# A decode step fed by one load queue: first load cut by partitions, x turned by TensorE, wo in five pieces

## The chip, the cores and the metric

The kernel runs on one core of a Trainium2 chip. The metric is device time in microseconds (us), the median of several executions. A core has five engines that run side by side: TensorE (PE in the profile; its weight loads are PEld), VectorE (DVE), ScalarE (ACT), GpSimd (POOL) and SyncE (SP), which here only issues loads. Loads are carried out by 16 DMA engines.

## The reference, cut to what matters

One token (x has 576 numbers) goes through two mixers whose outputs are added to x. All tensors are bfloat16.

```
xn = layernorm(x)
# A: attention over the last W = 4096 of 65536 cached positions, 32 query heads, 16 KV heads of 128
q  = xn @ wq                              # [576] x [576, 4096]
p  = softmax(q . k_cache[last W] / sqrt(128));  o = p . v_cache[last W]
A  = o @ wo                               # [4096] x [4096, 576]
# B: gated MLP
z  = gelu(xn @ w_in)                      # [576] x [576, 4608];  z1, z2 = halves
B  = (z1 * (w_sp * layernorm(z2) + b_sp)) @ w_out
out = x + A + B
```

What is read: 33.6 MB of K and V, 4.7 MB wq, 5.3 MB w_in, 2.7 MB w_out and 4.7 MB wo. Each byte is used once.

## The kernel before, in words

**The loads.** Every large load is issued by SP in the order of the program (lines 99 to 111): wq in two tiles of 5 and 4 half rows per partition; K0 and K1; w_in in three tiles; then K2 to K7 alternating with V0 to V5; V6, V7; w_out; wo in pieces of 10, 8, 6, 4, 2 and 2 rows per partition. A K or V tile (`load_kv`) is two heads, 128 partitions of 16 KB each. All tiles come from one ring of seven buffers (`ring`), so a load waits until the reader of an earlier tile in its buffer is done. Besides, transfers report their landing on eight counters that are used in turn, and a load waits until the transfer before it on its counter has landed. SP issues in order: a load that waits holds all behind it.

**x.** ScalarE's queue issues four small loads (lines 114 to 120): x as 64 partitions of 9 numbers (`x64`), x as one row (`xrow`, used at the end to add x to the output), and two scalars (`spb`). PE spreads x64 over 128 partitions by a matmul with a 0/1 matrix `rmat` that POOL copies from the identity (lines 137 and 194), so that partition p holds the nine numbers of p // 2. Lines 197 to 219 compute the layernorm and write `XT`.

**The work.** With XT, 36 matmuls give q (`qps`, L227); copies, matmuls and scalings lay it out as `Qb` (L236 to L255). Then a loop goes over sixteen half tiles of K, four per group: VectorE transposes half a K tile (`t_half`, L268), PE computes scores (`s_half`, L277); after each group VectorE takes the maximum (L298), ScalarE the exponentials (L305), VectorE and ScalarE transpose them (L315, L321), and PE multiplies with V (`pv`, L344). The MLP's input matmuls (L380) run after the first group. At the end the last group's output is normalised and laid out as `Y` (L354 to L372), and matmuls add w_out's and wo's products to two accumulators (L467), wo's pieces in the order in which they land. Two casts and one store end the program (L492 to L494). The order on each engine is that of the program text.

Of the kernel before, what the change touches and what calls it, by code (L numbers as in the profile page):

```python
# [9 lines left out]
BF16 = mybir.dt.bfloat16  # L10
# [4 lines left out]
D = 576  # L15
# [3 lines left out]
SK = 65536  # L19
W = 4096  # L20
# [6 lines left out]
TP = 2 * NT  # L27
# [7 lines left out]
NS = 9  # L35
# [4 lines left out]
def kernel(  # L40
# [14 lines left out]
    nc = tc.nc  # L55
    P = nc.NUM_PARTITIONS
# [4 lines left out]
    const = ctx.enter_context(tc.tile_pool(name="const", bufs=1))  # L61
# [10 lines left out]
    x_flat = A_x.flatten_outer_dims()  # L72


    def ring_tile(name, rows, width):
        t = ring.tile([P, SLOT], BF16, name=name, tag="ring")
        return t[:, 0:rows * width].rearrange("p (s c) -> p s c", c=width)

    def load_halves(src, lo, n, name):

        v = ring_tile(f"{name}{lo}", n, src.shape[1] // 2)
        rows = src.rearrange("r (e c) -> (r e) c", e=2).rearrange("(p s) c -> p s c", s=NS)
        nc.sync.dma_start(v, rows[:, lo:lo + n, :])
        return [(lo + s, v[:, s, :]) for s in range(n)]

    def load_kv(src, m, name):

        t = ring.tile([P, SLOT], BF16, name=f"{name}{m}", tag="ring")
        v = t[:, 0:TP * DH]
        nc.sync.dma_start(v, src[0, 2 * m:2 * m + 2, SK - W:SK, :].rearrange("h (r t) d -> r h (t d)", t=TP))  # L90
        return v.rearrange("p (t d) -> p t d", d=DH)

    def load_n(src, per, lo, n, name):
        v = ring_tile(f"{name}{lo}", n, D)
        nc.sync.dma_start(v, src.rearrange("(p t) n -> p t n", t=per)[:, lo:lo + n, :])
        return [(lo + t, v[:, t, :]) for t in range(n)]

    K, V = {}, {}
    wq_sb = load_halves(A_wq, 0, 5, "wq") + load_halves(A_wq, 5, 4, "wq")
    for m in range(2):  # L100
        K[m] = load_kv(A_k_cache, m, "k")
    win_sb = sum((load_halves(B_w_in, lo, 3, "win") for lo in (0, 3, 6)), [])
    for m in range(2, NP):
        K[m] = load_kv(A_k_cache, m, "k")
        V[m - 2] = load_kv(A_v_cache, m - 2, "v")
# [1 line left out]
        V[m] = load_kv(A_v_cache, m, "v")  # L107
    wout_sb = load_n(B_w_out, NF, 0, NF, "wout")
    wo_sb = []
    for n in (10, 8, 6, 4, 2, 2):  # L110
        wo_sb += load_n(A_wo, 32, len(wo_sb), n, "wo")


    x64 = const.tile([64, NS], BF16, name="x64")
    nc.scalar.dma_start(x64[:], x_flat.rearrange("o (m j) -> (o m) j", j=NS))
    xrow = const.tile([1, D], BF16, name="xrow")
    nc.scalar.dma_start(xrow[:], x_flat)
    spb = const.tile([1, 2], BF16, name="spb")
    nc.scalar.dma_start(spb[:, 0:1], B_w_sp.flatten_outer_dims()[0:1, 0:1])
    nc.scalar.dma_start(spb[:, 1:2], B_b_sp.flatten_outer_dims()[0:1, 0:1])  # L120


    ident = const.tile([P, P], BF16, name="ident")
# [7 lines left out]
    ones_b = const.tile([1, P], BF16, name="ones_b")  # L131
    nc.vector.memset(ones_b[:], 1.0)
    ps_x = ps_m.tile([P, 512], FP32, name="ps_x", tag="m")
    nc.vector.memset(ps_x[:], 0.0)
    qps = ps_a.tile([P, 512], FP32, name="qps", tag="a")
    nc.vector.memset(qps[:], 0.0)
    rmat = const.tile([64, P], BF16, name="rmat")
    nc.gpsimd.tensor_copy(rmat[:].rearrange("p (r h) -> p r h", h=2),
                          ident[0:64, 0:64].unsqueeze(2).to_broadcast([64, 64, 2]))
    mask = const.tile([P, 2], FP32, name="mask")  # L140
    nc.vector.reduce_sum(mask[:], ident[:].rearrange("p (r h) -> p h r", h=2), axis=AXX)
    mask4 = const.tile([P, 4], FP32, name="mask4")
# [32 lines left out]
    for n in range(2):  # L175
        t = const.tile([P, TP, 16, 2], BF16, name=f"pz{n}")
# [3 lines left out]
    for n in range(2):  # L180
        t = ps_s.tile([P, 2, 512], FP32, name=f"S{n}")
# [9 lines left out]
    nc.gpsimd.memset(mb[:], 0.0)  # L191


    nc.tensor.matmul(ps_x[:, 0:NS], lhsT=rmat[:], rhs=x64[:], start=True, stop=True)  # L194
    x_col = const.tile([P, NS], FP32, name="x_col")
    stat = const.tile([P, 2], FP32, name="stat")
    nc.vector.tensor_copy(x_col[:], ps_x[:, 0:NS])
# [27 lines left out]
    for s, wv in wq_sb:  # L225
        for g in range(4):
            nc.tensor.matmul(  # L227
                qps[32 * g:32 * g + 2, :], lhsT=XT[:, s, :], rhs=wv[:, 512 * g:512 * (g + 1)],
                start=(s == 0), stop=(s == NS - 1), tile_position=(0, 32 * g),
# [12 lines left out]
    for k in range(4):  # L242
        for be in range(4):
            nc.tensor.matmul(
                qps2[:, k, be, :].rearrange("p (r g) -> p r g", r=2),
                lhsT=q_rep[0:NR, 2 * k + be // 2, be % 2].rearrange("p a d -> p (a d)"),
                rhs=idq, start=True, stop=True)
# [181 lines left out]
    for j in range(2 * NP):  # L429
        g, o = divmod(j, GK)  # L430
# [7 lines left out]
        if g > 0 and o == 1:  # L438
            if g > 1:
                sm_b(g - 1)  # L440
            else:
# [3 lines left out]
                for n, pool in enumerate((ps_a, ps_b)):  # L445
                    t = pool.tile([P, 512], FP32, name=f"acc{n}", tag="ab"[n])
                    acc.append(t[32 * n:32 * n + 1, 0:CW])
                    nc.tensor.matmul(acc[n], lhsT=ones_b[:, 0:1], rhs=xrow[:, CW * n:CW * (n + 1)],
                                     start=True, stop=False, tile_position=(0, 32 * n))
# [75 lines left out]
```

## Time and profile before

| | |
|---|---|
| median of 3 runs | 127.74 us (127.64 to 127.87) |
| profiled execution | 127.7 us, span 125.9 us |
| busy in the span | PE 67.8 us, DVE 77.3, ACT 33.6, POOL 8.2 |
| read from memory | 50.96 MB, 405 GB/s over the span |
| DMA packets | 4127, 534 of them under 512 B |
| x64: issued, landed, first use | 0.74, 9.27, 9.40 us |
| XT ready, first qps matmul | 13.03 us |
| last K tile landed | 90.96 us |
| Y written | 116.67 us |
| last wo piece landed | 122.83 us |

The span runs from the first to the last recorded instruction; the run's time has 1.8 us more around it. The page has strips of 40 equal slices of 3.15 us: a digit is the busy share of a slice in tenths, and below the DMA line stands what was moved in GB/s. The chain of waits is read from the last instruction backwards, each step to what released it. "SPq" is SP's queue: the time in which it issues a load. A row of the waits gives who waited for whom, the total in us, how many times, and the longest.

### The profile page before, as it was taken

How to read it: one execution, taken by the hardware profiler on the slowest of the kernel's cores; microseconds unless marked ns; L12 is line 12 of the kernel's file. 1: busy time of each engine (PE TensorE's matmuls, PEld its weight loads, DVE VectorE, ACT ScalarE, POOL GpSimd, SP SyncE). 2: the span in 40 equal slices, each digit the busy share in tenths (PEclk: the TensorE clock that was granted, in tenths of full speed). 3: DMA queues.
4: the chain of work that ended last, by engine and by line, in shares of the span. 5: the costliest groups of instructions: out<-in, count | busy, mean ns of one | idle time of the engine just before them, and what ended most of it. 6: DMA issues, size and time to landing. Idle time of an engine off the chain costs nothing.

```text
span 125.9 us, 1614 instructions
## 1 busy us (share of the span) xinstructions
PE 67.8 (54%) x618; PEld 30.9 (25%) x618; DVE 77.3 (61%) x149; ACT 33.6 (27%) x85; POOL 8.2 (7%) x28
## 2 busy tenths in 40 slices
PE   0002841089999977069356049648039711187861
PEld 0001301021299922014111012411012511024530
DVE  6704135999353896793898298899098967005001
ACT  1200011000036590000441930260950183910001
POOL 3991000000000000100000000000000000000000
PEclk9999999999996557856999959967756995559999
DMA  4999999999999999999999999999999999999950
GB/s 130 417 427 437 432 422 442 419 426 433 435 429 427 442 416 416 437 437 432 437 422 432 437 427 432 432 416 437 437 424 437 427 426 453 409 416 415 419 226 0
DMA packets 4127, 51.06 MB, mean 406 GB/s; under 512 B 534, under 2 KB 536, under 8 KB 1048
## 3 DMA queue, kind: packets, MB, share of 16 engines
q1 hardware_dynamic: 4034, 50.96, 95.3%
q8 instruction: 5, 0.08, 0.2%
q10 hardware_dynamic: 86, 0.00, 0.0%
q14 instruction: 2, 0.02, 0.0%
HBM read 50.96 MB, written 0.00 MB: 405 GB/s over the span
## 4 chain that ended last, share of the span: by engine, by line
DMA 56%; PE 16%; DVE 14%; ACT 7%; issue 3%; SPq 1%; POOL 0%; ACTq 0%
DMA k<-in_A_k_cache_dram 43%; DMA x<-in_A_x_dram 7%; DMA wo<-in_A_wo_dram 7%; DVE kT L268 6%; PE ops L344 6%; PE S L277 5%; ACT PT L321 4%; PE qps L227 3%; ACT pz L305 2%; DVE Qb L255 2%; DVE pt L315 2%; DVE q_rep L238 1%; ACT q_rep L236 1%; DVE on L358 1%; PE lps L327 1%
## 5 line engine op out<-in xcount | busy, mean ns | idle before, releaser
L277 PE MATMUL S<-kT,Qb 128*8 128x512 bf16 x128 | 32.5, 638 | 29.0 <-DVE kT L268 29.0
L268 DVE STREAM_TRANSPOSE kT<-k 128x1024 f32<-128x1024 f32 x32 | 36.9, 1212 | 6.9 <-DMA k<-in_A_k_cache_dram 6.8
L305 ACT ACTIVATE pz<-S,nm 64x1024 bf16<-64x1024 f32 x8 | 11.3, 1409 | 45.1 <-DVE nm L301 30.4
L321 ACT COPY PT<-pt 32x64 f32<-32x64 f32 x64 | 18.9, 296 | 14.3 <-DVE pt L315 13.6
L277 PEld LDWEIGHTS <-Qb 128*8 128x8 bf16 x128 | 6.4, 96 | 48.4 <-issue 45.4
L344 PE MATMUL ops<-v,PT 128*16 128x512 bf16 x128 | 11.7, 451 | 3.5 <-ACT PT L321 3.5
L315 DVE STREAM_TRANSPOSE pt<-pz 128x1024 bf16<-128x1024 bf16 x8 | 9.4, 1214 | 4.2 <-ACT pz L305 4.2
L380 PEld LDWEIGHTS <-win 128*128 128x128 bf16 x162 | 10.1, 169 | 0.9 <-issue 0.9
L380 PE MATMUL zps<-XT,win 128*128 128x2 bf16 x162 | 10.2, 202 | 0.0
L354 DVE SCALAR_TENSOR_TENSOR om<-ops,rs,dmask 128x512 f32<-128x512 f32 x4 | 3.0, 742 | 7.1 <-PE ops L344 7.1
L298 DVE TENSOR_REDUCE mx<-S 128x1 f32<-128x1024 f32 x4 | 4.9, 1222 | 3.8 <-PE S L277 3.8
L344 PEld LDWEIGHTS <-PT 128*16 128x16 bf16 x128 | 5.0, 98 | 7.4 <-ACT PT L321 4.1
L467 PE MATMUL acc<-wo,Y 128*1 128x288 bf16 x64 | 4.7, 285 | 1.7 <-DMA wo<-in_A_wo_dram 1.6
L194 PE MATMUL ps_x<-x,rmat 64*128 64x9 bf16 x1 | 0.2, 164 | 9.4 <-DMA x<-in_A_x_dram 9.4
L236 ACT CAST q_rep<-qps 128x512 bf16<-128x512 f32 x2 | 1.2, 585 | 14.7 <-DVE q_rep L238 14.7
L227 PE MATMUL qps<-wq,XT 128*2 128x512 bf16 x36 | 4.0, 626 | 1.0 <-DVE XT L218 1.0
L492 DVE CAST res<-acc 1x288 bf16<-1x288 f32 x1 | 0.4, 446 | 6.6 <-PE acc L467 6.6
L358 DVE TENSOR_REDUCE on<-om 128x128 f32<-128x512 f32 x4 | 4.1, 1036 | 0.1
L238 DVE CAST q_rep<-qps 128x512 bf16<-128x512 f32 x2 | 1.4, 692 | 4.6 <-PE qps L227 3.9
L327 PE MATMUL lps<-lx,lsum 128*128 128x1 f32 x8 | 2.2, 343 | 3.2 <-DVE Y L372 3.2
L493 ACT CAST res<-acc 1x288 bf16<-1x288 f32 x1 | 0.4, 389 | 12.7 <-PE acc L467 12.7
L467 PEld LDWEIGHTS <-Y 128*1 128x1 bf16 x64 | 2.8, 83 | 3.4 <-issue 2.5
(90 smaller groups left out, 44.6 us busy)
## 6 DMA issues: line engine op xcount, KB each, us to landing
k<-in_A_k_cache_dram SPq DMA_DIRECT2D x8, 2048.0 KB, 24.3
v<-in_A_v_cache_dram SPq DMA_DIRECT2D x8, 2048.0 KB, 24.8
win<-in_B_w_in_dram SPq DMA_DIRECT2D x3, 1728.0 KB, 23.3
wout<-in_B_w_out_dram SPq DMA_DIRECT2D x1, 2592.0 KB, 30.6
wq<-in_A_wq_dram SPq DMA_DIRECT2D x1, 2560.0 KB, 8.7
wq<-in_A_wq_dram SPq DMA_DIRECT2D x1, 2048.0 KB, 13.0
wo<-in_A_wo_dram SPq DMA_DIRECT2D x1, 1440.0 KB
wo<-in_A_wo_dram SPq DMA_DIRECT2D x1, 1152.0 KB
```

What stands on the lines that cost most here:

```text
L227: nc.tensor.matmul(qps[32 * g:32 * g + 2, :], lhsT=XT[:, s, :], rhs=wv[:, 512 * g:512 * (g + 1)], start=(s == 0), stop=(s == NS - 1), tile ...
L268: nc.vector.transpose(dst[:, 1024 * n:1024 * (n + 1)], src[:, 1024 * n:1024 * (n + 1)])
L277: nc.tensor.matmul(S[g % 2][32 * i:32 * i + 8, hf, :], lhsT=Qb[:, 2 * m + hd, be].rearrange("p a h -> p (a h)"), rhs=kv[:, be // 2, be % 2 ...
L298: nc.vector.tensor_reduce(out=mx[:, 0:1], in_=s[:], op=ALU.max, axis=mybir.AxisListType.XY)
L305: nc.scalar.activation(p[lo:hi, :, :, hd], s[lo:hi].rearrange("p a (t r) -> p (a t) r", r=16), ACT.Exp, bias=nm[lo:hi, 0:1], scale=SCALE, ...
L315: nc.vector.transpose(dst[:, 1024 * n:1024 * (n + 1)], src[:, 1024 * n:1024 * (n + 1)])
L321: nc.scalar.copy(PT4[32 * a:32 * a + 32, i % 2, i // 2, :], pt4[32 * i:32 * i + 32, :, a])
L327: nc.tensor.matmul(lps[:, 0:1], lhsT=lsum[:].rearrange("p q c x h -> p (q c x h)"), rhs=lx[:, g:g + 1], start=True, stop=True)
L344: nc.tensor.matmul(ops[32 * q:32 * q + 16, :], lhsT=d["PT"][:, pr, t0:t0 + 4].rearrange("p t x h -> p (t x h)"), rhs=V[2 * g + pr][:, t0:t ...
L358: nc.vector.reduce_sum(on[:], om[:].rearrange("p c d -> p d c"), axis=AXX)
L380: nc.tensor.matmul(zps[:, :, t], lhsT=wt[:, t, :], rhs=XT[:, s, :], start=(s == 0 and t == 0), stop=(s == NS - 1 and t == NF - 1), skip_gr ...
L467: nc.tensor.matmul(acc[n], lhsT=lhs[:, col:col + 1], rhs=wv[:, CW * n:CW * (n + 1)], start=False, stop=last, tile_position=(0, 32 * n))
```

## The change

- The first wq load has two half rows per partition, not five, and goes out in four transfers by partitions: every eighth from 0, every eighth from 4, every fourth from 2, every second from 1 (16, 16, 32, 64 partitions). The next wq loads have four and three half rows.
- `xrow` and the two scalars are issued by SP between the second and the third wq load. ScalarE's queue issues no load. `x64` and `rmat` are gone: VectorE copies xrow into `xtw`, one partition with 9 x 64 x 2 numbers, and nine matmuls with one column each spread it over the partitions.
- K0, K1 and the three w_in tiles go out in two transfers each, the even and the odd partitions.
- wo comes in pieces of 14, 9, 5, 3 and 1.
- The program has 40 transfers in place of 33. The loads' order of tiles, the ring and all later work stay; there are three wq tiles now, so the last w_in tile is the eighth in the ring.

```diff
-    def load_halves(src, lo, n, name):
+    def load_halves(src, lo, n, name, parts=((0, 1),)):
         v = ring_tile(f"{name}{lo}", n, src.shape[1] // 2)
         rows = src.rearrange("r (e c) -> (r e) c", e=2).rearrange("(p s) c -> p s c", s=NS)
-        nc.sync.dma_start(v, rows[:, lo:lo + n, :])
+        for p0, step in parts:
+            nc.sync.dma_start(v[p0:P:step], rows[p0:P:step, lo:lo + n, :])
...
-    def load_kv(src, m, name):
+    def load_kv(src, m, name, step=1):
...
-        nc.sync.dma_start(v, src[0, 2 * m:2 * m + 2, SK - W:SK, :].rearrange("h (r t) d -> r h (t d)", t=TP))
+        rows = src[0, 2 * m:2 * m + 2, SK - W:SK, :].rearrange("h (r t) d -> r h (t d)", t=TP)
+        for hd in range(step):
+            nc.sync.dma_start(v[hd:P:step], rows[:, hd:2:step, :])
...
-    wq_sb = load_halves(A_wq, 0, 5, "wq") + load_halves(A_wq, 5, 4, "wq")
+    wq_sb = load_halves(A_wq, 0, 2, "wq", ((0, 8), (4, 8), (2, 4), (1, 2)))
+    wq_sb += load_halves(A_wq, 2, 4, "wq")
+    xrow = const.tile([1, D], BF16, name="xrow")
+    nc.sync.dma_start(xrow[:], x_flat)
+    spb = const.tile([1, 2], BF16, name="spb")
+    nc.sync.dma_start(spb[:, 0:1], B_w_sp.flatten_outer_dims()[0:1, 0:1])
+    nc.sync.dma_start(spb[:, 1:2], B_b_sp.flatten_outer_dims()[0:1, 0:1])
+    wq_sb += load_halves(A_wq, 6, 3, "wq")
     for m in range(2):
-        K[m] = load_kv(A_k_cache, m, "k")
-    win_sb = sum((load_halves(B_w_in, lo, 3, "win") for lo in (0, 3, 6)), [])
+        K[m] = load_kv(A_k_cache, m, "k", 2)
+    win_sb = sum((load_halves(B_w_in, lo, 3, "win", ((0, 2), (1, 2))) for lo in (0, 3, 6)), [])
...
-    for n in (10, 8, 6, 4, 2, 2):
+    for n in (14, 9, 5, 3, 1):
         wo_sb += load_n(A_wo, 32, len(wo_sb), n, "wo")
-    x64 = const.tile([64, NS], BF16, name="x64")
-    nc.scalar.dma_start(x64[:], x_flat.rearrange("o (m j) -> (o m) j", j=NS))
...
-    rmat = const.tile([64, P], BF16, name="rmat")
-    nc.gpsimd.tensor_copy(rmat[:].rearrange("p (r h) -> p r h", h=2),
-                          ident[0:64, 0:64].unsqueeze(2).to_broadcast([64, 64, 2]))
...
-    nc.tensor.matmul(ps_x[:, 0:NS], lhsT=rmat[:], rhs=x64[:], start=True, stop=True)
+    xtw = const.tile([1, NS, D // NS, 2], BF16, name="xtw")
+    nc.vector.tensor_copy(xtw[:], xrow[:].rearrange("p (m j) -> p j m", j=NS).unsqueeze(3).to_broadcast([1, NS, D // NS, 2]))
+    for j in range(NS):
+        nc.tensor.matmul(ps_x[:, j:j + 1], lhsT=xtw[:, j].rearrange("p m h -> p (m h)"), rhs=ones_b[:, 0:1],
+                         start=True, stop=True)
```

More of the change, by code (lines that the diff above doesn't have):

```diff
@@ L109 @@
     wo_sb = []
-    for n in (10, 8, 6, 4, 2, 2):
+    for n in (14, 9, 5, 3, 1):
         wo_sb += load_n(A_wo, 32, len(wo_sb), n, "wo")
-    x64 = const.tile([64, NS], BF16, name="x64")
[L115 to L120, printed above, removed]
     ident = const.tile([P, P], BF16, name="ident")
```

## The prediction

> **What bounds the kernel now.** I read the strip of the page first, then the DMA rate by stage, then the chain of waits, and last the idle time of VectorE and of the load queue. The strip:
>
> ```profile
> DVE  6704135999353896793898298899098967005001
> DMA  4999999999999999999999999999999999999950
> GB/s 130 417 427 437 432 422 442 419 426 433 435 429 427 442 416 416 437 437 432 437 422 432 437 427 432 432 416 437 437 424 437 427 426 453 409 416 415 419 226 0
> ```
>
> No engine is busy in all slices, but the DMA engines are, from slice 1 to slice 37. The same by stage (columns: stretch, its length, busy us and instructions of PE, PEld, DVE, ACT, POOL, clock, DMA share, GB/s):
>
> ```profile
> 0.00:2.20 2.20, 0.00 (x0) 0.00 (x0) 1.21 (x6) 0.00 (x0) 0.98 (x7) 1.00 0.53 130
> 2.20:4.00 1.80, 0.00 (x0) 0.00 (x0) 1.59 (x8) 1.28 (x1) 1.02 (x5) 1.00 0.65 262
> 4.00:116.00 112.00, 62.18 (x535) 27.43 (x535) 73.87 (x135) 31.93 (x83) 6.21 (x18) 0.82 1.01 429
> 119.00:120.75 1.75, 0.88 (x18) 0.50 (x13) 0.00 (x0) 0.00 (x0) 0.00 (x0) 1.00 1.00 402
> 120.75:122.50 1.75, 1.24 (x18) 0.58 (x13) 0.00 (x0) 0.00 (x0) 0.00 (x0) 1.00 0.38 145
> 122.50:126.00 3.50, 0.51 (x6) 0.09 (x3) 0.45 (x1) 0.39 (x1) 0.00 (x0) 1.00 0.00 0
> ```
>
> The reader is to see one stream of 51 MB at 429 GB/s with a ragged head (until 4.0 us), a ragged end (from 120.75 us) and 3.4 us after it. The chain of waits says the same: long DMA steps that began long before they landed, then a short tail.
>
> ```profile
> 27.63 24.48 DMA k<-in_A_k_cache_dram
> ...
> 61.53 29.44 DMA k<-in_A_k_cache_dram
> ...
> 114.34 8.49 DMA wo<-in_A_wo_dram
> 122.83 0.04 issue
> 122.87 0.45 PE acc L467 x4
> 123.33 0.43 DVE res L492
> ```
>
> A 2 MB load takes 4.9 us at 429 GB/s; 24 to 29 us from issue to landing is time spent behind other loads. So a load may be issued later without harm, and only three things move the end: when the stream gets to full rate, its rate, and the work after the last landing.
>
> **The change, part by part.** The sum is made against the profiled execution's own 127.7 us (span 125.9, 1.8 around it); the median of the timed runs, 127.74, is the same.
>
> **The first load in four parts.** The head of before, in the timeline:
>
> ```profile
> 0.73 0.87 SPq L83 DMA_DIRECT2D wq<-in_A_wq_dram  x2
> 0.74 0.54 ACTq L115 DMA_DIRECT2D x<-in_A_x_dram  x1
> 1.31 0.68 ACTq L117 DMA_DIRECT2D xrow<-in_A_x_dram  x1
> 2.02 0.21 ACTq L119 DMA_DIRECT2D spb<-in_B_w_sp_dram  x1
> 2.27 0.33 ACTq L120 DMA_DIRECT2D spb<-in_B_b_sp_dram  x1
> ```
>
> In steps of 0.1 us no bytes appear before 1.7 us, and the first 15 packets (20 KB, one partition each) are spread from 1.7 to 2.2 us. By 4.0 us 130 x 2.2 + 262 x 1.8 = 0.76 MB have moved, which the full rate does in 1.76 us: the stream is as good as started at 2.24 us. A first part of 16 partitions gives each of 16 DMA engines one packet of 8 KB at once. Best end: full rate from where the first packets were, and earlier by what a shorter issue saves (0.41 us for a 128-partition load; the shortest issue shown is 0.21): 2.24 - 1.5 = 0.74 us gained. Worst end: each part still takes 0.41 us to issue while the two 16-partition parts carry 0.131 MB each, 0.31 us of stream. Then the engines run dry 0.1 us twice, and the late first packets stay: nothing gained. I take 0.3 us, the mean spread of the first packets (0.25 of the 0.5 us) and a little of the shorter issue.
>
> **Three tiny loads on SP, none on ScalarE's queue.** The 64-partition load of x goes. xrow and the two scalars now stand on SP ahead of the third wq load, both K loads and win: by the rows above 0.68 + 0.21 + 0.33 = 1.2 us of issue. The 3.1 MB of wq issued before them are 7.3 us of stream, which covers this. If that cover were gone, the 1.2 us would count in full.
>
> **New waits in SP's order.** In both programs each load waits until the transfer eight before it has landed, because completions are counted on eight counters. That is why win was issued only at 9.28 us in before. In the changed order the second half of K1 waits for the 2 MB wq load and win's first half for xrow, about 9.5 to 10 us. Behind them all of SP's queue waits. Issued and not moved by then are wq's last 1.57 MB, K0's 2.10 and half of K1, 1.05: 4.7 MB, 11 us of stream. The last win tile is now the eighth ring tile and waits for the first wq tile to be read by PE, about 16 us, when some 15 us are queued. Nothing.
>
> **K0, K1 and win in halves of every second partition.** Five more transfers, whose issue (0.41 to 0.66 us each) lies beside the stream. Each packet is still one partition's row of 14 or 16 KB and each engine still gets an equal share. The trace of before has no large load on 64 partitions. One bound is nothing, or a little less than nothing if the shorter parts smooth the stream: its best slice ran at 453 GB/s, which over 9.5 MB would be 1.2 us gained. The other is the slowest full stretch shown, 402 GB/s, where wo's packets of 4.6 to 6.9 KB go: 9.5 MB take 23.6 us and not 22.1, 1.5 us lost. I take nothing: the row with the nearest packet size is 4 to 116 us, at 429.
>
> **x from one row, by PE.** xrow lands behind 3.1 MB: 2.0 + 7.3 = 9.3 us and some latency, 9.8, against 9.27 for x now. Then a DVE copy of 1152 elements on one partition: the 512-element cast of L238 is 0.69 us and the 9-element copy 0.17, so 0.17 + 1152 x 0.00103 = 1.36. Then nine weight loads with nine one-column matmuls: the sixteen pairs of L244 take 0.60, so 0.34 and 0.16 to the end of the last, 0.5, where now 0.3 stand. x_col is read at about 9.8 + 0.1 + 1.4 + 0.5 = 11.8 and not 9.6, and Qb, the first transposes and the first scores come 2.2 us later (1.4 to 3.5). What covers that:
>
> ```profile
> SPq L90 <- DMA k<-in_A_k_cache_dram: 10.4, 3, 4.5
> DVE kT L268 <- DMA k<-in_A_k_cache_dram: 6.8, 5, 2.9
> PE acc L467 <- DMA wo<-in_A_wo_dram: 1.6, 3, 0.9
> ```
>
> The third K tile's buffer comes free at 27.6 us now, 29.8 then, but its turn in the stream is at 18.4 MB, 45 us. VectorE's five waits for K hold 6.8 us; the longest, 2.9 us, ends with the last K at 90.96 us. A delay under 2.9 us is gone there, since K7 lands when the stream brings it. Past that there is a second cover: from Y (116.7 us) PE needs 64 x 0.066 = 4.2 us for wo and would end at 121.1, but ends at 123.3 for lack of data, 2.2 us. Cost: nothing until the delay passes about 5 us.
>
> **rmat is not built.** One POOL copy of 0.28 us less at 1.4 us, where POOL waits for VectorE next anyway. Nothing.
>
> **wo in 14, 9, 5, 3, 1.** The last landing is followed by two matmuls and not four. At 0.066 us each that is 0.13 us; were each as long as a quarter of the last four (0.45), 0.22. The low end is none, if the three-row piece lands so close ahead that its six matmuls (0.4 us) end last. I take 0.13. The last piece is issued into a ring place freed by V6 in place of V7; both come free at about 114 us, and its turn in the stream is near 122. The larger first piece (16 KB packets, not 11.5) and the smaller last ones (3.5 and 1.2 KB, not 2.3) pull the rate both ways; I set 0, between 0.1 and -0.1.
>
> **Sum:** 127.7 - 0.3 - 0.13 = 127.27, so **127.3 us**.
>
> **Rivals.**
>
> *The halves slow the stream (slower).* Place: 14 to 36 us, where K0, K1 and win pass. How 64 partitions are shared among the 16 DMA engines no row shows, and two engines may then meet at one place of the memory. For it: the stream is the bound, so every lost byte counts and nothing hides it; no row shows such a load. Against it: packet size and share per engine stay. At 402 GB/s, 127.27 + 1.5 = 128.8. It decides from a rate 2% lower there (22.1 x 0.02 = 0.44, the whole gain).
>
> [...]
>
> [...]
>
> *The later x reaches the end (slower).* If xrow lands only after all of wq (4.7 MB, 3.7 us later than taken), the delay is 5.9 us, 0.9 over the cover: 128.2. Against it: it is issued ahead of the last wq load.
>
> **How the numbers follow.** Forecast 0.53 (127.3; alone 126.7 to 127.5), no gain at the head 0.16 (127.7), halves slower 0.25 (128.8), late x 0.06 (128.2). About 0.2%, 0.25 us, is what a measurement can tell from no change. The forecast's upper edge and the second rival make "same" 0.16, the other two 0.31 slower, the rest faster. The low edge is 0.74 + 0.22 of gain, 126.7; the high edge the slower rival at 128.8.
>
> **What would show it.** In the changed profile the GB/s of the first two slices should be above 130 and 417; first packets near 1.5 us and no hole after them; the stretch 14 to 36 us still near 430 GB/s (it is 430 now); the first qps matmuls near 15 us, not 13.03; the last K landing near 90.7; two matmuls after the last wo landing. I am wrong if 14 to 36 us falls below 420 GB/s, if a hole opens at 2 to 4 us, or if VectorE no longer waits for the last K.

## The result and the profile after

The changed kernel takes 130.56 us (median of 6 runs, 130.04 to 131.44), the kernel before 127.63 in the same comparison. The ratio is 1.0232, 95% interval 1.021 to 1.0255: 2.9 us slower, where 0.4 us faster was forecast. The profiled execution took 131.3 us, span 129.3; it is among the longer ones of the six, so differences read from it come out larger than those of the medians. Where the executions of one kernel lie over 1.5% apart, its ratio is taken from those near the shortest.

The strip of the changed kernel's page:

```profile
DMA  2989999999999999999999999999999999999930
GB/s 81 294 284 408 431 449 421 421 431 428 430 422 445 421 421 446 416 431 436 431 431 431 436 426 421 446 431 421 441 428 416 441 440 431 409 436 416 412 138 1
```

A slice is 3.23 us here, 3.15 before. Among the slices in which the stream runs, the first four alone differ: 81, 294, 284, 408 against 130, 417, 427, 437. From slice 4 on the rate is as before, and the last K tile lands 3.7 us later (94.67 against 90.96 us). The table by stage, changed kernel (columns as in the prediction):

```profile
0.00:2.20 2.20, 0.00 (x0) 0.00 (x0) 1.21 (x6) 1.28 (x1) 0.70 (x6) 1.00 0.08 22
2.20:4.00 1.80, 0.00 (x0) 0.00 (x0) 1.59 (x8) 0.00 (x0) 1.02 (x5) 1.00 0.71 191
4.00:6.00 2.00, 0.00 (x0) 0.00 (x0) 1.65 (x3) 0.00 (x0) 1.94 (x13) 1.00 1.00 365
6.00:8.00 2.00, 0.00 (x0) 0.00 (x0) 0.00 (x0) 0.00 (x0) 2.00 (x2) 1.00 0.81 233
8.00:10.00 2.00, 0.00 (x0) 0.00 (x0) 0.00 (x0) 0.00 (x0) 1.16 (x3) 1.00 0.87 311
10.00:12.00 2.00, 0.00 (x0) 0.00 (x0) 0.00 (x0) 0.00 (x0) 0.00 (x0) 1.00 1.03 430
14.00:36.00 22.00, 10.20 (x86) 3.69 (x88) 14.71 (x41) 1.17 (x2) 0.55 (x1) 0.77 1.01 432
120.00:122.00 2.00, 2.00 (x38) 1.43 (x33) 0.17 (x1) 0.00 (x0) 0.00 (x0) 1.00 0.99 416
122.00:124.00 2.00, 0.98 (x18) 0.58 (x14) 0.00 (x0) 0.00 (x0) 0.00 (x0) 1.00 0.76 304
124.00:126.00 2.00, 1.32 (x20) 0.69 (x15) 0.00 (x0) 0.00 (x0) 0.00 (x0) 1.00 0.22 81
```

The same stretches before:

```profile
4.00:6.00 2.00, 0.00 (x0) 0.00 (x0) 1.66 (x3) 0.00 (x0) 1.94 (x13) 1.00 1.03 440
6.00:8.00 2.00, 0.00 (x0) 0.00 (x0) 0.00 (x0) 0.00 (x0) 2.00 (x2) 1.00 1.01 430
8.00:10.00 2.00, 0.16 (x1) 0.10 (x1) 0.36 (x4) 0.00 (x0) 1.17 (x3) 1.00 0.96 406
14.00:36.00 22.00, 13.54 (x110) 4.68 (x99) 14.68 (x30) 1.17 (x2) 0.00 (x0) 1.00 1.01 430
```

Three things to read. From 4 to 6 us the DMA share is 1.00 at 365 GB/s, where before has 1.03 at 440: packets take longer, the engines are not idle. The hole from 6 to 10 us lies in the time in which the second wq load passes, a whole one of 128 partitions; 1.05 MB of parts had gone by 6 us. There some engines are idle (shares 0.81 and 0.87), although the third wq load had been issued by 5.23 us and K0's first half began to be at 5.27:

```profile
4.87 0.36 SPq L84 DMA_DIRECT2D wq<-in_A_wq_dram  x1
5.27 9.21 SPq L93 DMA_DIRECT2D k<-in_A_k_cache_dram  x4
```

From 14 to 36 us, where the halves of K0, K1 and w_in go, the rate is 432, against 430 before.

The chain of waits of the changed kernel begins with the issues, which are long, and ends with the last wo landing:

```profile
0.73 0.62 SPq L84
1.36 0.06 issue
1.42 0.57 SPq L84
...
3.93 9.53 DMA xrow<-in_A_x_dram
13.46 0.02 issue
13.48 1.35 DVE xtw L195
14.83 0.05 issue
14.88 0.41 PE ps_x L197 x9
...
126.06 0.04 issue
126.11 0.70 PE acc L471 x8
```

An issue of a part takes about 0.6 us, whether it has 16 or 64 partitions. xrow landed at 13.46 us. Eight matmuls, not two, follow the last landing that PE waits for: those of the three-row piece and those of the last, one-row piece.

### The profile page after: what moved, and what is told of

Its sections match the earlier page's. It is cut to its first block, busy times and chain, and to the rows that moved or that the text cites. A ratio compares the mean times of both kernels' runs of the same rounds, so it can differ in the third digit from the quotient of the medians.

```text
span 129.3 us, 1645 instructions
## 1 busy us (share of the span) xinstructions
PE 67.0 (52%) x626; PEld 31.0 (24%) x626; DVE 78.4 (61%) x150; ACT 33.6 (26%) x85; POOL 7.9 (6%) x27
## 4 chain that ended last, share of the span: by engine, by line
DMA 46%; issue 31%; PE 10%; DVE 7%; SPq 3%; POOLq 0%; POOL 0%
DMA k<-in_A_k_cache_dram 22%; DMA wo<-in_A_wo_dram 17%; DMA xrow<-in_A_x_dram 7%; PE S L281 4%; PE ops L348 3%; DVE kT L272 3%; SPq L84 2%; DVE xtw L195 1%; DVE on L362 1%; PE lps L331 1%; PE acc L471 1%; DVE om L358 1%; PE ps_x L208 0%; POOLq L524 0%; POOL mv L214 0%
## 5 line engine op out<-in xcount | busy, mean ns | idle before, releaser
L281 PE MATMUL S<-kT,Qb 128*8 128x512 bf16 x128 | 32.5, 639 | 27.7 <-DVE kT L272 27.6
L384 PEld LDWEIGHTS <-win 128*128 128x128 bf16 x162 | 10.1, 165 | 0.9 <-issue 0.9
L195 DVE COPY xtw<-xrow 1x1152 bf16<-1x1152 bf16 x1 | 1.3, 1342 | 7.6 <-DMA xrow<-in_A_x_dram 7.6
L231 PE MATMUL qps<-wq,XT 128*2 128x512 bf16 x36 | 3.4, 549 | 1.9 <-DVE XT L222 1.9
```

Of the source, the lines that this page charges most:

```text
L281: nc.tensor.matmul(S[g % 2][32 * i:32 * i + 8, hf, :], lhsT=Qb[:, 2 * m + hd, be].rearrange("p a h -> p (a h)"), rhs=kv[:, be // 2, be % 2 ...
L384: nc.tensor.matmul(zps[:, :, t], lhsT=wt[:, t, :], rhs=XT[:, s, :], start=(s == 0 and t == 0), stop=(s == NS - 1 and t == NF - 1), skip_gr ...
```

## The experiments

The theories, with their letters in the expectations. **Parts** (P): the four parts of the first load cost the time. **Small loads** (S, until e4): the three tiny loads on SP make the hole. **Halves** (H): K0, K1 and w_in in halves. Then, among theories of the parts: **narrow** (N, later W and port, and N16, for which the parts of 16 alone are slow; their packets are slow because of the partitions they write), **issue** (I; 0.6 us each, carrying too little) and **collision** or **start** (C, later small, from e13 on S; a start in several transfers puts the engines out of step); a last one, **read**, blames the rows that are read. A part or load is called strided when it takes every n-th partition.

**e1, the first wq tile in one transfer**, all else as changed.

```diff
-    wq_sb = load_halves(A_wq, 0, 2, "wq", ((0, 8), (4, 8), (2, 4), (1, 2)))
+    wq_sb = load_halves(A_wq, 0, 2, "wq")
```

> The changed kernel with the first wq tile (two half rows) loaded by one transfer of 128 partitions; all else as changed. Theory P (the four parts starve and slow the head): the hole until 10 us closes, 2.2 us or more come back of the 2.9 lost, so about 128.0 us, and the rate from 4 to 10 us is near 430 GB/s. Theory S (the three tiny loads on SP's queue make the hole from 6 to 10 us, where the second wq load passes): only the late head, some 0.9 us, comes back, 129.6 us, and 6 to 10 us stays near 270 GB/s. Theory H (the halves of K0, K1 and win): nothing comes back, 130.5 us.

Measured: 127.55 us, ratio to before 0.9993 (0.9983 to 1.0003). The whole loss is gone. The table by stage of e1:

```profile
2.20:4.00 1.80, 0.00 (x0) 0.00 (x0) 1.59 (x8) 0.00 (x0) 1.02 (x5) 1.00 0.88 341
4.00:6.00 2.00, 0.00 (x0) 0.00 (x0) 1.65 (x3) 0.00 (x0) 1.94 (x13) 1.00 1.06 451
6.00:8.00 2.00, 0.00 (x0) 0.00 (x0) 0.00 (x0) 0.00 (x0) 2.00 (x2) 1.00 1.03 442
8.00:10.00 2.00, 0.00 (x0) 0.00 (x0) 0.00 (x0) 0.00 (x0) 1.16 (x3) 1.00 0.94 400
120.00:122.00 2.00, 1.49 (x26) 0.93 (x21) 0.00 (x0) 0.00 (x0) 0.00 (x0) 1.00 0.62 240
122.00:124.00 2.00, 0.82 (x12) 0.33 (x7) 0.45 (x1) 0.39 (x1) 0.00 (x0) 1.00 0.02 8
```

The same second wq load, at 6 to 8 us, now moves at 442 GB/s. So the parts slow what comes behind them.

**e2, the parts alone in the kernel before** (wq in tiles of 2, 4, 3 half rows, the first in four parts; x as before).

```diff
-    wq_sb = load_halves(A_wq, 0, 5, "wq") + load_halves(A_wq, 5, 4, "wq")
+    wq_sb = load_halves(A_wq, 0, 2, "wq", ((0, 8), (4, 8), (2, 4), (1, 2)))
+    wq_sb += load_halves(A_wq, 2, 4, "wq") + load_halves(A_wq, 6, 3, "wq")
```

> The kernel before with one thing changed: wq in tiles of 2, 4 and 3 half rows, the first of them in the four parts. The tiny loads stay on ScalarE's queue. Theory P: about 130 us, with a rate near 270 GB/s from 6 to 10 us. Theory S: about 128.5 us, only the start of the stream is later (first packets at 1.9 us and 200 GB/s until 3 us). Theory H: 127.6 us.

Measured: 131.01 us, 1.0266 (1.0228 to 1.0303). The parts do it without the tiny loads on SP. Theory small loads falls.

**e3, K0, K1 and w_in whole** in the changed kernel.

```diff
-        K[m] = load_kv(A_k_cache, m, "k", 2)
+        K[m] = load_kv(A_k_cache, m, "k")
-    win_sb = sum((load_halves(B_w_in, lo, 3, "win", ((0, 2), (1, 2))) for lo in (0, 3, 6)), [])
+    win_sb = sum((load_halves(B_w_in, lo, 3, "win") for lo in (0, 3, 6)), [])
```

> The changed kernel with K0, K1 and the three w_in tiles each in one transfer of 128 partitions. Theories P and S: nothing of the hole before 10 us goes, since these loads come after it: 130.2 to 130.6 us. Theory H: the stretch behind 10 us and the ragged end of the stream (122 to 126 us, against 120.5 to 122.5 before) get shorter, 129.5 us or less.

Measured: 130.60 us, as the changed kernel's 130.56. The halves cost nothing (e1 has them too and equals before); theory halves falls.

**e4, the wo pieces alone** in the kernel before.

```diff
-    for n in (10, 8, 6, 4, 2, 2):
+    for n in (14, 9, 5, 3, 1):
```

> The kernel before with wo in pieces of 14, 9, 5, 3 and 1 and nothing else. All theories: within 0.3 us of before. By the prediction's sum 0.13 us less, 127.5 us; if the pieces lengthen the ragged end of the stream, up to 1 us more, 128.6 us.

Measured: 127.46 us, 0.9985 (0.9975 to 0.9994): 0.2 us faster, as a term of the sum, though not for the reason given. Its chain ends

```profile
122.32 0.04 issue
122.36 0.70 PE acc L467 x8
123.06 0.44 DVE res L492
```

The tail after the last wait is longer (0.70 us against 0.45), but it starts 0.5 us earlier (122.32 against 122.83; this profiled execution is e4's shortest, 127.32 us). The wait is for the three-row piece: the one-row piece, issued at 113.99 us, lands 8.7 us later, near 122.7, while PE works through the other. This is the case for which the prediction set the gain at none.

Next, what in the parts is slow.

**e5, parts as blocks of neighbours**, K0, K1 and w_in whole.

```diff
-            nc.sync.dma_start(v[p0:P:step], rows[p0:P:step, lo:lo + n, :])
+            nc.sync.dma_start(v[p0:p1], rows[p0:p1, lo:lo + n, :])     # (0, 16), (16, 32), (32, 64), (64, 128)
```

> The changed kernel with the four parts of the first wq tile as blocks of neighbouring partitions (0-15, 16-31, 32-63, 64-127), K0, K1 and w_in whole. [...] Theory I (four issues of 0.6 us that carry too little): 130.5 us as with strided parts. Theory C (a start in parts sets the DMA engines out of step and they collide until some 8 us after the start, whatever partitions they write): 130 to 130.6 us.

Measured: 129.96, 130.04, 134.01 and 134.17 us, ratio 1.0178 (1.0158 to 1.0198). They spread too far to rank blocks against strided parts, but the trace of the 129.96 us execution shows another kind of loss:

```profile
0.73 2.51 SPq L84 DMA_DIRECT2D wq<-in_A_wq_dram  x5
4.00:6.00 2.00, 0.00 (x0) 0.00 (x0) 1.66 (x3) 0.00 (x0) 1.94 (x13) 1.00 0.98 217
6.00:8.00 2.00, 0.00 (x0) 0.00 (x0) 0.00 (x0) 0.00 (x0) 2.00 (x2) 1.00 1.11 311
```

The four blocks and the next wq load take 0.50 us each to issue, the first packet comes at 1.75 us, as with a whole load, and from 4 to 8 us the engines are full at 217 and 311 GB/s. With blocks the loss is slow packets, not issues or idle engines.

**e6, two halves at the head**; **e8, four pieces by columns at the head**, each with all 128 partitions.

```diff
-... "wq", ((0, 8), (4, 8), (2, 4), (1, 2)))
+... "wq", ((0, 2), (1, 2)))                                   # e6
+for c in (0, 1024):                                            # e8
+    for s in range(2):
+        nc.sync.dma_start(v[:, s:s + 1, c:c + 1024], rows[:, s:s + 1, c:c + 1024])
```

> The changed kernel with the first wq tile in two transfers, even and odd partitions, in place of four. Theory N: 64 partitions are not narrow, 127.6 us. Theory I: one further issue of 0.6 us that carries 0.52 MB, 1.2 us of stream, so nothing runs dry: 127.6 to 127.9 us. Theory C: part of the loss, 128.3 to 129.5 us, with packets slower than their nominal time until some 4 to 8 us.

> The changed kernel with the first wq tile in four transfers by columns: each 128 partitions with a quarter of the row (2 KB packets). Theory N: 128 partitions are never narrow, about 127.7 us. Theory I: four issues as now, of which each carries 0.26 MB, 0.61 us of stream, so about 0.3 us is lost against one transfer: 127.9 us. Theory C: the engines start in parts, up to 130 us.

Measured: 128.40 us (1.0049, 1.0033 to 1.0066) and 129.43 us (1.0132, 1.0114 to 1.015). Both lose against e1, 0.85 and 1.9 us, though none of their transfers has under 64 partitions. Of e8's loss 0.24 us is the size of its packets: 512 of 2 KB take 0.084 us each, and an eighth of a 16 KB packet's 0.61 is 0.076. So the head suffers from a start in several transfers, narrow or not.

**e7, the four parts in mid-stream**: K2 to K5 of the kernel before, each in 16, 16, 32 and 64 partitions.

```diff
-        nc.sync.dma_start(v, rows)
+        nc.sync.dma_start(v[0:P:8], rows[0:P // 2:4, 0:1, :])
+        nc.sync.dma_start(v[4:P:8], rows[2:P // 2:4, 0:1, :])
+        nc.sync.dma_start(v[2:P:4], rows[1:P // 2:2, 0:1, :])
+        nc.sync.dma_start(v[1:P:2], rows[:, 1:2, :])
```

> The kernel before with K2, K3, K4 and K5 each loaded in the same four parts (16, 16, 32, 64 partitions), while the stream is full. [...] Theories I and C: nothing, 127.5 to 127.9 us.

Measured: 136.63 us, 1.0692 (1.0649 to 1.0735), 2.2 us for each tile. Its table by stage, over the first two of the four tiles:

```profile
30.00:34.00 4.00, 3.72 (x19) 0.87 (x16) 1.96 (x3) 0.00 (x0) 0.00 (x0) 1.00 1.00 429
34.00:38.00 4.00, 4.00 (x68) 4.00 (x68) 2.06 (x6) 1.62 (x3) 0.00 (x0) 0.85 1.07 347
46.00:50.00 4.00, 3.57 (x16) 0.78 (x15) 3.56 (x9) 0.92 (x4) 0.00 (x0) 0.50 1.06 299
```

The share is 1.07 and 1.06 at 347 and 299 GB/s: engines full, packets slow. In the trace's packet records 265 of the 16 KB packets are over 1.3 times the usual time, 1.05 us on average against 0.61 for all others; the parts of 16, 16 and 32 partitions of four tiles have 256. The 64-partition parts and the V tiles behind run at 0.61. What the 265 take beyond 0.61 us is, over 16 engines, 7.4 of the 8.6 us that the profiled execution (136.26 us) is longer than before's.

**e9, K2 to K5 in quarters of every fourth partition**; **e10, in halves of neighbours** (0-63, 64-127); **e11, the parts of e7 read from neighbouring rows**; **e12, in four pieces by columns**. The lines are shortened; in each run they stand for K2 to K5 alone.

```diff
-        nc.sync.dma_start(v, rows)
+        for q in range(4): nc.sync.dma_start(v[q:P:4], rows[q // 2:P // 2:2, q % 2:q % 2 + 1, :])          # e9
+        for q in range(2): nc.sync.dma_start(v[64 * q:64 * q + 64], rows[32 * q:32 * q + 32])              # e10
+        nc.sync.dma_start(v[0:P:8], rows[0:16, 0:1, :])                                                    # e11
+        nc.sync.dma_start(v[4:P:8], rows[16:32, 0:1, :])
+        nc.sync.dma_start(v[2:P:4], rows[32:64, 0:1, :])
+        nc.sync.dma_start(v[1:P:2], rows[:, 1:2, :])
+        for q in range(4): nc.sync.dma_start(v[:, 2048 * q:2048 * q + 2048], rows[:, :, 2048 * q:2048 * q + 2048])  # e12
```

> The kernel before with K2 to K5 each in four transfers of every fourth partition (32 each). With the parts of 16, 16, 32 and 64, about 64 packets of a tile (as many as the three narrow parts have) took about 1.0 us in place of 0.61. [...] Theory W (parts under 64 partitions are slow): all 128 packets of a tile, twice the loss of the four parts, about 145 us.

> The kernel before with K2 to K5 each in two transfers of 64 neighbouring partitions (0-63, 64-127). [...] Theories read (the source addresses of the parts collide) and small (any smaller transfer puts the engines out of step): 127.7 us, as with even and odd halves.

> The kernel before with K2 to K5 in parts of 16, 16, 32 and 64 written to the same partitions as before (every eighth from 0 and 4, every fourth from 2, every second from 1), but read from neighbouring rows of the source: rows 0-15, 16-31, 32-63 of the first head, then the second head. The keys of a head are thereby in another order than the values, so the output is not the reference's; the work is the same. Theory port or W (what is written decides): as with the strided rows, 136 to 137 us. Theory read: 128 us.

> The kernel before with K2 to K5 each in four transfers by columns: all 128 partitions, a quarter of the row each (4 KB packets). Theories port, W and read: 127.7 us, since every transfer is as wide as now. Theory small: slow packets here too, 130 us or more. If it is 127.7, what the split by columns cost at the head (1.7 us) is a matter of the start and not of the split.

Measured: 128.15 (1.0034, 1.0024 to 1.0044), 163.92 (156.53 to 166.56, no interval), 137.93 (1.0797, 1.0741 to 1.0853) and 129.15 us (1.0114, 1.0099 to 1.013). Stretches of e9 (its profiled execution is its shortest, 127.70 us) and then of e10 (its longest, 166.56 us):

```profile
34.00:38.00 4.00, 4.00 (x64) 3.81 (x62) 2.13 (x6) 1.25 (x1) 0.00 (x0) 0.96 1.01 426
46.00:50.00 4.00, 3.53 (x18) 0.90 (x13) 2.96 (x13) 1.35 (x5) 0.00 (x0) 0.76 1.00 426
```

```profile
34.00:38.00 4.00, 4.00 (x64) 3.85 (x63) 2.13 (x6) 1.29 (x1) 0.00 (x0) 1.00 1.15 330
38.00:42.00 4.00, 4.00 (x68) 4.00 (x67) 2.27 (x2) 1.68 (x4) 0.00 (x0) 0.62 0.96 205
42.00:46.00 4.00, 2.37 (x39) 2.37 (x38) 0.11 (x1) 3.71 (x13) 0.00 (x0) 0.50 0.99 209
```

Thirty-two partitions four apart run at the usual rate, 426 GB/s at shares of 1.01 and 1.00; sixty-four neighbours at 205 and 209, half the rate, with shares of 0.96 and 0.99. The written partitions decide, and not the source: e11, which reads neighbouring rows, is not faster than e7 but 1.3 us slower, with 318 slow packets. The rates leave part of e10's loss over: by an estimate from them a tile of 2.10 MB takes 10.1 us at 207 GB/s and 4.9 at 429, 5.2 more, but the tiles lose 7 us each in the shortest run and 9 by the median. e10's trace has 752 slow packets, though the four tiles have 512, so at least 240 packets of the unsplit loads between them run slow too.

In e7 the part of 32, of the same kind as in e9, was slow, but it stood right behind the two of 16. Whether they made it slow is not shown, since no run has something between them.

Last, how the head divides.

**e13, four parts of 32 at the head**; **e14, three parts of 32, 32, 64**; **e15, the second wq load of the kernel before in the four parts**.

```diff
-... "wq", ((0, 8), (4, 8), (2, 4), (1, 2)))
+... "wq", ((0, 4), (2, 4), (1, 4), (3, 4)))      # e13
+... "wq", ((0, 4), (2, 4), (1, 2)))              # e14
-load_halves(A_wq, 5, 4, "wq")
+load_halves(A_wq, 5, 4, "wq", ((0, 8), (4, 8), (2, 4), (1, 2)))   # e15
```

> The changed kernel with the first wq tile in four transfers of 32 partitions, every fourth from 0, 2, 1 and 3: as many issues as changed, and no part under 32. [...] Theory S (a start in several transfers costs, since each issue takes 0.6 us, whatever its width): 129.5 to 130.5 us.

> The changed kernel with the two 16-partition parts put into one of 32, so 32, 32 and 64. Theory N16: 128 us. Theory S: between the two halves (128.4) and the four parts (130.5), 129 to 129.5 us.

> The kernel before with its second wq load (four half rows, 16 KB packets) in the parts of 16, 16, 32 and 64, behind the first 2.6 MB, so when the stream already runs. Theory N16: as one K tile in the middle, 8.9 / 4 = 2.2 us more, 129.9 us. Theory S: the four issues of 0.6 us lie under 6 us of stream, 127.7 us.

Measured: 130.32 (1.0172, 1.0124 to 1.0219), 129.84 (1.0179, 1.0155 to 1.0203) and 129.39 us (1.0133, 1.0109 to 1.0157). Without any 16-partition part the head loses nearly as much. With the first tile in 1, 2, 3 and 4 transfers the changed kernel takes 127.55, 128.40, 129.84 and 130.3 to 130.6 us. In a running stream (e15) the four parts cost 1.7 us. So at the head a start in several transfers costs most of the loss even without a 16-partition part (e13 and e14 come near S's figures), and in a running stream the narrow parts do (e15 comes near N16's 129.9, not S's 127.7).

From the packet records, the mean of 16 DMA engines over 11 us after the first packet (usual time: a packet's size at 26.8 GB/s, what a 16 KB packet in 0.61 us is):

| kernel | first packet at, us | usual time | slow beyond it | idle |
|---|---|---|---|---|
| before | 1.77 | 10.22 | 0.57 | 0.22 |
| e1, one transfer | 1.77 | 10.32 | 0.47 | 0.21 |
| e6, two halves | 2.08 | 9.90 | 0.85 | 0.25 |
| e14, three parts | 2.10 | 9.36 | 1.13 | 0.51 |
| e13, four of 32 | 2.10 | 8.10 | 1.94 | 0.96 |
| changed | 2.14 | 8.00 | 1.65 | 1.34 |
| e8, columns | 1.76 | 9.03 | 1.43 | 0.55 |
| e5, four blocks | 1.75 | 7.9 | 3.0 | 0.1 |

Against e1 the changed kernel's first packet is 0.37 us later, its packets are slower by 1.18 us and its engines idle 1.13 us longer: 2.7 of the 3.7 us between the two profiled executions. The rest shows at the ragged end (304 and 81 GB/s from 122 to 126 us, against 240 and 8 from 120 to 124). That engines which fell behind at the head make the end so is the author's reading and is not shown. The late first packet goes with strided parts: blocks (e5) and columns (e8) start as early as a whole load and still lose.

**e16, a version from the parts that are harmless**: the kernel before with wq whole in tiles of 2, 4 and 3 half rows, and the wo pieces.

```diff
-    wq_sb = load_halves(A_wq, 0, 5, "wq") + load_halves(A_wq, 5, 4, "wq")
+    wq_sb = load_halves(A_wq, 0, 2, "wq") + load_halves(A_wq, 2, 4, "wq") + load_halves(A_wq, 6, 3, "wq")
-    for n in (10, 8, 6, 4, 2, 2):
+    for n in (14, 9, 5, 3, 1):
```

> The kernel before with wq in tiles of 2, 4 and 3 half rows, each in one transfer, and wo in pieces of 14, 9, 5, 3 and 1; x by ScalarE's queue as before. All theories: the smaller first packets start the stream up to 0.2 us earlier and the wo pieces are worth 0.2 us as they were alone, so 127.2 to 127.5 us.

Measured: 127.71 us, 0.9997 (0.9988 to 1.0006): no gain, and outside the 127.2 to 127.5 expected. The smaller tile starts nothing earlier (first packet at 1.74 us), and the wo pieces, worth 0.2 us in e4, bring nothing here; why is open. The shortest version is e4, 0.15% under before.

## Why the prediction was wrong

- **What bounds the kernel**: right. One stream, and the end moves with it: in the profiles the last K lands 3.7 us later and the execution ends 3.6 us later.
- **The first load in four parts: this step failed.** It was set at 0.3 us gained, between 0.74 and nothing. It cost 3.0 us (changed against e1). The lower end was not a bound: it took 0.41 us for an issue from a whole load, while a strided part took 0.57 to 0.62; it took the packets at their usual rate; and it let the loss end with the parts. In place of that the runs show first packets at 2.14 us, not near 1.5, engines idle between the parts and again from 6 to 10 us, and slow packets that go on through the second wq load. The prediction's own sign of being wrong, a hole at 2 to 4 us, was there: 191 GB/s from 2.2 to 4.0 us, where before has 262. Why unsplit loads behind the parts run slow stays open.
- **No gain at the head (127.7 us, chance 0.16)**: no run shows a head in four parts that costs next to nothing. They cost 3.0 us there, and in mid-stream 2.2 us a tile (e7), where the 32-partition part behind the two narrow ones is slow too. Nor is narrowness the main matter at the head: e13 has no part under 32 partitions and loses 2.2 us by its ratio, 2.6 by its median, where the changed kernel loses 2.9. How much of the changed kernel's head is narrowness and how much the start in four can't be told apart better than this.
- **The halves of K and w_in at nothing**: right (e1, e3, and 432 GB/s from 14 to 36 us). The slower rival named the wrong place.
- **The later x**: the size was off, the cover right. xrow landed at 13.46 us, not 9.8, because the stream was late, and the first qps matmuls came at 18.73 and not 15. In e1 it landed at 10.24 and the first qps matmuls came at 15.53, near the forecast. The copy took 1.35 us (1.36 set), the nine matmuls 0.41 (0.5 set). VectorE still waits for the last K:

```profile
DVE kT L272 <- DMA k<-in_A_k_cache_dram: 6.0, 3, 2.8
```

  The longest wait is 2.8 us, where before has 2.9. The first qps matmuls were 5.7 us late and the last K 3.7, because of the stream; the 2.0 us between them were gone by then. (The load issued at 27.6 us before, which the prediction calls the third K tile, is the fourth; the 18.4 MB ahead of it are right.)
- **Tiny loads on SP, SP's new waits, rmat**: nothing, right (e1 has them all and equals before).
- **wo**: 0.13 us set; 0.2 measured in e4, nothing in e16. The mechanism was wrong, so that e4's figure comes near is luck: not two but eight matmuls follow the last wait, and in e4 that wait ends earlier.

## What to carry to other kernels

Where one load stream sets the time, start it with one transfer over all 128 partitions: each further strided transfer of the first tile cost 0.5 to 1.4 us here, and the saving that a small first part promises didn't appear. If a tile must be split by partitions in a running stream, take every second (e1 and e3, at no cost) or every fourth (e9, 0.1 us a tile); halves of neighbours and parts with every eighth partition cost 2 to 9 us a tile here. A DMA share of 1.0 or more at a rate below the usual 430 GB/s (1.07 at 347 in e7) went with slow packets here, 1.05 us in place of 0.61, and it is to be told from a share below 1.0 at a low rate (0.81 at 233 in the changed kernel), in which engines are idle. That need not mean that nothing was issued: from 6 to 10 us the changed kernel had shares of 0.81 and 0.87 with later loads already issued.

## What was not expected of the hardware

A strided first part starts 0.3 us later than a whole load (2.08 to 2.14 us against 1.77), and its issue and that of the whole wq load right behind it take 0.6 us; blocks of neighbours do neither (e5). The loss in e10 is well over what 207 GB/s for four tiles gives (29 us in the shortest run, 36 by the median, against 4 x 5.2 = 21). Pieces by columns, which keep all 128 partitions, cost 1.5 us in mid-stream (e12). Its 2048 packets of 4 KB take 0.159 us each, where a quarter of a 16 KB packet is 0.153, which is 0.8 us over 16 engines; 0.65 us is one episode of slow packets, 4 us long, at the first of the four tiles. What starts that episode, and the rest of the 1.9 us at the head (e8 against e1), is open. Open too is why whole loads behind a split one run slow: in the changed kernel 18 packets of the second wq load, begun between 5.6 and 9.0 us, take 0.81 to 1.91 us, where 0.61 is usual.
